# Gate and up of a spectral GEGLU block: seven products of halves instead of eight, for 256 of 448 channels and three of seven tile pairs

## The chip, the cores and the metric

The kernel runs on one core of a Trainium2 chip. The metric is the device time of one execution in microseconds (us). The engines are named as in the profile: PE is the matrix engine (PEld its weight loads), DVE the vector engine, ACT the scalar engine, POOL the GpSimd engine, SP the engine whose queue issues the transfers.

## What is computed

The input `x` has 8192 tokens of 448 channels, all in float32. `c` and `w_mod` give six rows of 448 numbers (`sa, ca, ga, sb, cb, gb`). `A` is a spectral mixer: a Fourier transform over the 8192 tokens, a small two-layer network on each frequency, and the inverse transform. `B` is a gated feed-forward network with 1792 hidden channels.

```python
h = _layernorm(x) * (1 + ca) + sa
x = x + ga * A(h)                       # rfft2, two blockwise layers, shrink, irfft2
h = _layernorm(x) * (1 + cb) + sb
x = x + gb * ((_gelu(h @ w_gate) * (h @ w_up)) @ w_down)
```

## The kernel before

The first 385 us hold the forward transform, the frequency network and the first half of the inverse transform. The rest is one loop, and the change lies in it. It has 32 iterations `i`, each over two blocks of 128 tokens. The last half of the inverse transform, the residual, the second norm and the packing of a later iteration's tokens are spread over an iteration as hooks.

An iteration has 14 steps `k` of gate and up. Step `k` computes gate and up of one tile of 128 hidden channels: `t = k // 2`, and `q = k % 2` picks tile `t` or tile `t + 7`, so a tile pair is two steps. Numbers are split into a high and a low float16 part, and a product takes high by high, high by low and low by high. The 448 channels make three tiles of 128 and one of 64, which makes 20 matmuls of 256 columns (two blocks of 128 tokens) in a step, `gu` at L1087. Two consecutive tile pairs share eight more matmuls with 64 rows: the first of the two (the "first pair") gets its results out only at its second step, after these; the second pair gets them out step by step. Since there are seven tile pairs, the odd `t` are first pairs in odd iterations and the even `t` in even iterations.

`gate_up_out` takes a result out of the accumulation bank: ACT computes the gelu of the gate half (L1123), DVE multiplies it with the up half (L1128). After both tiles of a pair POOL makes four sums of the four quarters (L1134 to L1137), since the down projection takes seven products of halves in place of eight. `quantize`, called at odd `k` for the pair before, rounds the seven operands: ACT the high part (L1145), DVE the low part (L1146).

After `k == 2` comes `down(i - 1)`: 147 matmuls of 224 columns (L1153 to L1155), with copies out by ACT (L1176, L1182), adds by DVE (L1177 to L1194), and on POOL an add (L1190) and four passes that finish the output (L1167, L1168).

The hooks for iteration `i + 2` are: at `k = 3` the inverse's inputs `g` and `v` are split into two float32r parts, the high one by ACT (L105), the low one by POOL (L107); at `k = 6` the inverse's six matmuls (L987 to L989); at 7 the residual, at 8 the statistics, at 9 and 10 the inverse square root in small DVE steps, at 11 and 12 the norm on DVE, at 13 the packing to float16. At `k = 0` SP issues the 16 transposing transfers of iteration `i + 1`.

Each engine takes its instructions in the order in which the Python code calls them; nothing reorders them. So what stands ahead of an instruction on its engine can be read from the code.

Of the kernel before, what the change touches and what calls it, by code (L numbers as in the profile page):

```python
# [19 lines left out]
D = 448  # L20
F = 1792
# [16 lines left out]
NTT = len(PKO)  # L38
LAM = 0.01
# [6 lines left out]
def spectral_geglu(ctx, tc, x, w1, b1, w2, b2, wg, wu, wd, cvec, wmod, cf1, cs2, cmi, cgm, out):  # L46
# [272 lines left out]
    with ExitStack() as bctx:  # L319
# [359 lines left out]
        def row_scales():  # L679

            GL.tensor_scalar(cb_r, cb_r, 1.0, None, op0=ALU.add)
            tiny.extend([free] * 2)
            for j, r in enumerate((cb_r, sb_r)):
                VL.tensor_reduce(rmax[:, j : j + 1], r, mybir.AxisListType.X, ALU.max, apply_absolute_value=True)
            bnd = cpool.tile([128, 1], F32, name="hb")
            VL.scalar_tensor_tensor(bnd, rmax[:, 0:1], 21.2, rmax[:, 1:2], op0=ALU.mult, op1=ALU.add)
            VL.tensor_scalar(bnd, bnd, 1.01, 1e-30, op0=ALU.mult, op1=ALU.add)
            pow2(sk, bnd)
            GL.tensor_scalar(sb_r, sb_r, sk, None, op0=ALU.mult)
            GL.tensor_scalar(cb_r, cb_r, sk, None, op0=ALU.mult)  # L690
# [48 lines left out]
        def scales1():  # L739
# [20 lines left out]
            pow2(sw, mxa)  # L760
# [122 lines left out]
        def load_g(i):  # L883
            g = ep.tile([128, CB, 128], F32, tag="g", name="g")
            dma(g, cgm[:, i * CB : (i + 1) * CB, :])
            xx = ep.tile([128, CB, D], F32, tag="xx", name="xx")
            dma(xx, xv[:, i * CB : (i + 1) * CB, :])
            nxt.setdefault(i, {}).update({"g": g, "xx": xx})
# [22 lines left out]

        def split_g(i):
            gh = ep.tile([128, CB, 128], F32R, tag="gh", name="gh")
            gl = ep.tile([128, CB, 128], F32R, tag="gl", name="gl")
            split(gh, gl, nxt[i]["g"], el=G)
            nxt[i]["g"] = gh, gl
# [32 lines left out]
    with ExitStack() as cctx:  # L949
# [7 lines left out]

        def load_d8(t):
            load_d(t, *(cp2.tile([128, n, HC], F32, tag=f"dr{n}", name="dr", bufs=2) for n in (3, 4)))
# [8 lines left out]
        def split_v(i, cs=slice(0, D)):  # L968
            n = nxt[i]
            if "vh" not in n:  # L970
                n["vh"] = cp.tile([128, CB, D], F32R, tag="vh", name="vh")
                n["vl"] = cp.tile([128, CB, D], F32R, tag="vl", name="vl")
            for b in each(i):
                split(n["vh"][:, b, cs], n["vl"][:, b, cs], n["v"][:, b, cs], el=G)

        def inverse(i, cs=slice(0, D), tag="pc"):
            nxt[i]["ps"] = []
            for b in range(CB):
                ps = bank(tag, "pi2")[:, cs]
                if i < 3:  # L980

                    T.matmul(ps, nxt[i]["g"][:, b], nxt[i]["v"][:, b, cs], start=True, stop=True)
                    nxt[i]["ps"].append(ps)
                    continue
                vh, vl = nxt[i]["vh"], nxt[i]["vl"]
                gh, gl = nxt[i]["g"]
                T.matmul(ps, gh[:, b], vh[:, b, cs], start=True, stop=False)  # L987
                T.matmul(ps, gl[:, b], vh[:, b, cs], start=False, stop=False)  # L988
                T.matmul(ps, gh[:, b], vl[:, b, cs], start=False, stop=True)  # L989
                nxt[i]["ps"].append(ps)  # L990

        def residual(i, cs=slice(0, D)):
# [3 lines left out]
            for b in range(CB):  # L996
# [34 lines left out]
        def norm2(i, b):  # L1031
            mvt, x1, r = nxt[i]["mv"], x1t[i], nxt[i]["r"][0]
            if b == 0:
                nxt[i]["n"] = cp.tile([128, CB, D], F32, tag="n2", name="n2")
            n = nxt[i]["n"]
# [9 lines left out]
        def pack_lo(i):  # L1045
# [6 lines left out]
            nts[i] = cp.tile([128, NTT, H], F16, tag="nt", name="nt", bufs=2)  # L1052
# [42 lines left out]

        def gate_up(i, k):
# [7 lines left out]
            seq = [(wh, j, j) for j in range(4)] + [(wh, j, j + 5) for j in range(3)] + [(wl, j, j) for j in range(3)]  # L1104
            for pr in range(2):
                for j, (w, tw, tn) in enumerate(seq):
                    gu(i, t, q, pr, w, full, tw, tn, first_pair and pr == 0 and j == 0, not first_pair and j == len(seq) - 1)
            if not first_pair:
                gate_up_out(i, t, q)
            elif q == 1:  # L1110
# [6 lines left out]
                for qq in range(2):  # L1117
                    gate_up_out(i, t, qq)
# [39 lines left out]
        def down(i):  # L1158
# [82 lines left out]
        }  # L1241
        inverse(0, halves[0], "pa")
# [32 lines left out]
        for i in range(nch):  # L1275
            for k in range(NFT):
# [7 lines left out]
                if i == 1:  # L1284
                    for fn, *args in second.get(k, []):
                        fn(2, *args)
                if k == 2 and i > 0:
                    down(i - 1)
                    if i == 1:
                        transposes_dma(2, range(2, NTT))  # L1290
                for fn, *args in first.pop(i * NFT + k, []):
                    fn(*args)
                if k == (3, 1, 0)[min(i, 2)] and i + 2 < nch:
                    load_v(i + 2)
                    load_g(i + 2)
                for d, fn, *args in hooks.get(k, []):
# [79 lines left out]
```

## Time and profile before

| | |
|---|---|
| time, median of 3 runs | 1942.13 us (1941.53 to 1943.13) |
| the profiled execution | 1942.27 us, its span 1940.5 us |
| PE busy | 98% of the span; weight loads 87% |
| DVE, ACT, POOL busy | 57%, 41%, 60% |
| granted PE clock, mean | 0.995 |
| gate and up, L1087 | 9856 matmuls, one of them 273 ns from start to end |
| down, L1153 to L1155 | 4704 matmuls, one of them 259 ns |

Matmuls follow each other in a pipeline, so the duration of one is longer than the distance from one start to the next; rates are read from the starts in the timeline. A row of the timeline gives the start, the length, the engine, the line, the operation, what is written and read, a count, and in brackets the idle time ahead of it and what ended that. A row of the groups gives a count, the total, the mean of one in ns, and the idle time ahead.

### The profile page before, as it was taken

The numbers are of one execution on the slowest core, as the hardware profiler recorded it, in microseconds if no ns is written. First come the engines' busy times: TensorE is split into PE (matmuls) and PEld (weight loads), VectorE is DVE, ScalarE is ACT, GpSimd is POOL, SyncE is SP. The second block draws the span as 40 slices with busy tenths as digits, with TensorE's granted clock in tenths as the row PEclk, the third lists the DMA queues.
The fourth block names the chain that finished last, engine by engine and source line by source line (L and its number), as shares of the span: only waits on it lengthen the run. The fifth ranks groups of instructions, "written<-read, shape, count | busy, mean of one in ns | idle before, by whom it ended". The sixth has DMA issues, their size and how long they took to land.

```text
span 1940.5 us, 43566 instructions
## 1 busy us (share of the span) xinstructions
PE 1901.1 (98%) x17636; PEld 1694.6 (87%) x17636; DVE 1108.7 (57%) x2352; ACT 790.1 (41%) x1342; POOL 1157.7 (60%) x1466
## 2 busy tenths in 40 slices
PE   7899999899999999999999999999999999999998
PEld 3599999778888888888888888888888888888897
DVE  8677788786555555555555555555555555555533
ACT  5587888553333333333333333333333333333322
POOL 3157655256666666666666666666666666666644
PEclk9899999999999999999999999999999999999999
DMA  9999777541111111111111111111111111111000
GB/s 351 313 286 261 194 195 196 166 125 48 44 44 44 43 43 43 43 43 44 43 44 43 43 44 43 44 44 42 45 43 44 44 43 44 43 44 44 21 16 20
DMA packets 167330, 163.35 MB, mean 84 GB/s; under 512 B 87252, under 2 KB 145496, under 8 KB 167128
## 3 DMA queue, kind: packets, MB, share of 16 engines
q1 hardware_dynamic: 167128, 160.57, 28.3%
q8 instruction: 138, 2.26, 0.5%
q14 instruction: 64, 0.52, 0.1%
HBM read 97.44 MB, written 47.25 MB: 75 GB/s over the span
## 4 chain that ended last, share of the span: by engine, by line
PE 86%; DVE 4%; ACT 3%; issue 3%; DMA 2%; POOL 1%; SPq 1%; ACTq 0%; POOLq 0%; DVEq 0%
PE pgu L1087 53%; PE pdn L1155 8%; PE pdn L1153 8%; PE pdn L1154 8%; PE ps L202 2%; DVE y L463 2%; PE pi L989 1%; PE pi L988 1%; PE pi L987 1%; POOL yl L107 1%; DVE st L163 1%; ACT th L105 0%; DMA raw<-in_B_w_gate 0%; POOL tl L107 0%; ACT zh L376 0%
## 5 line engine op out<-in xcount | busy, mean ns | idle before, releaser
L1087 PE MATMUL pgu<-nt,wh 128*128 128x256 f16 x6272 | 834.2, 273 | 0.1
L1087 PEld LDWEIGHTS <-wh 128*128 128x128 f16 x6272 | 602.7, 98 | 98.5 <-issue 31.0
L1123 ACT ACTIVATE gel<-pgu,dg 128x256 f32<-128x256 f32 x448 | 200.3, 473 | 793.2 <-PE pgu L1087 756.1
L1087 PE MATMUL pgu<-nt,wl 128*128 128x256 f16 (+1 forms) x3584 | 501.3, 272 | 0.6 <-DVE x L1128 0.6
L1155 PE MATMUL pdn<-wd,ac 128*128 128x224 f16 x1568 | 406.1, 259 | 0.2 <-DVE ac L1146 0.2
L1153 PE MATMUL pdn<-wd,ac 128*128 128x224 f16 x1568 | 406.1, 259 | 0.0
L1154 PE MATMUL pdn<-wd,ac 128*128 128x224 f16 x1568 | 406.1, 259 | 0.0
L1134 POOL TENSOR_TENSOR x<-x 128x128 f32<-128x128 f32 x223 | 239.9, 1076 | 264.0 <-DVE x L1128 230.5
L1146 DVE SCALAR_TENSOR_TENSOR ac<-x,sa_act,ac 128x896 f16<-128x896 f32 (+1 forms) x225 | 308.2, 1370 | 81.9 <-ACT ac L1145 81.9
L1087 PEld LDWEIGHTS <-wl 128*128 128x128 f16 (+1 forms) x3584 | 297.8, 97 | 57.6 <-issue 24.4
L1128 DVE TENSOR_TENSOR x<-pgu,gel 128x256 f32<-128x256 f32 x448 | 179.6, 418 | 278.7 <-ACT gel L1123 278.0
L1145 ACT ACTIVATE ac<-x,sa_act 128x896 f16<-128x896 f32 (+1 forms) x225 | 232.9, 1035 | 46.5 <-POOL x L1137 44.5
L1190 POOL TENSOR_TENSOR o<-u,p 128x224 f32<-128x224 f32 x32 | 21.0, 657 | 291.6 <-DVE u L1189 291.6
L1135 POOL TENSOR_TENSOR x<-x 128x128 f32<-128x128 f32 x223 | 158.1, 709 | 17.5
L1155 PEld LDWEIGHTS <-ac 128*128 128x128 f16 x1568 | 153.4, 98 | 0.5 <-DVE ac L1146 0.5
L1154 PEld LDWEIGHTS <-ac 128*128 128x128 f16 x1568 | 153.4, 98 | 0.4
L1153 PEld LDWEIGHTS <-ac 128*128 128x128 f16 x1568 | 153.4, 98 | 0.4
L107 POOL TENSOR_TENSOR yl<-y,yh 128x448 fp32r<-128x448 f32 x63 | 78.9, 1252 | 75.6 <-ACT yh L105 63.0
L463 DVE SCALAR_TENSOR_TENSOR y<-pm,t 64x224 f32<-64x224 f32 x256 | 99.5, 389 | 41.3 <-ACT t L455 37.4
L1136 POOL TENSOR_TENSOR x<-x 128x128 f32<-128x128 f32 x223 | 113.0, 507 | 0.0
L1137 POOL TENSOR_TENSOR x<-x 128x128 f32<-128x128 f32 x223 | 109.2, 490 | 0.0
L107 POOL TENSOR_TENSOR tl<-tr,th 128x896 f16<-128x896 f32 x30 | 57.3, 1909 | 69.5 <-DMA tr<-td 38.2
(281 smaller groups left out, 2728.4 us busy)
## 6 DMA issues: line engine op xcount, KB each, us to landing
tr<-td SPq DMA_DIRECT2D x64, 224.0 KB, 4.3
vd<-us SPq DMA_DIRECT2D x64, 224.0 KB, 3.3
xx<-in_A_x SPq DMA_DIRECT2D x32, 448.0 KB, 3.3
v<-vd SPq DMA_DIRECT2D x63, 224.0 KB, 2.7
out<-x SPq DMA_DIRECT2D x31, 448.0 KB, 2.6
xt<-in_A_x SPq DMA_DIRECT2D x15, 896.0 KB, 14.8
td<-xt SPq DMA_DIRECT2D x48, 224.0 KB, 4.3
nt<-pk SPq DMA_TRANSPOSE x480, 2.3
```

The lines of the kernel that those rows point to most:

```text
L107: (el or V).tensor_tensor(lo, src, h, ALU.subtract)
L463: V.scalar_tensor_tensor(y[ri * 64 : ri * 64 + 64, gi], pv[si, ri], LAM, tv[si, ri], op0=ALU.add, op1=ALU.min)
L1087: T.matmul(pgu[i, t, q][:, pr * H : (pr + 1) * H], w[rows, tw, f0 : f0 + 128], nts[i][rows, tn, :], start=start, stop=stop, skip_group_che ...
L1123: S.activation(gl, ps[:, :H], AF.Gelu_apprx_tanh, scale=dg)
L1128: V.tensor_tensor(dst, ps[:, H : 2 * H].rearrange("p (b c) -> p b c", b=2), gl.rearrange("p (b c) -> p b c", b=2), ALU.mult)
L1134: e.tensor_tensor(s1, a21, a22, ALU.add)
L1135: e.tensor_tensor(s2, s1, a11, ALU.subtract)
L1145: S.activation(ac[:, 0, k], x[:, k], AF.Copy, scale=sc)
L1146: V.scalar_tensor_tensor(ac[:, 1, k], x[:, k], sc, ac[:, 0, k], op0=ALU.mult, op1=ALU.subtract)
L1153: T.matmul(ps, ac[:, 0, ka], wds[t][:, 0, kb], start=t == 0, stop=False)
L1154: T.matmul(ps, ac[:, 0, ka], wds[t][:, 1, kb], start=False, stop=False)
L1155: T.matmul(ps, ac[:, 1, ka], wds[t][:, 0, kb], start=False, stop=t == NP - 1)
```

## The change

`SP = {2: 3, 4: 4, 6: 5}`: tile pairs 2, 4 and 6 take the new form from iterations 3, 4 and 5 on, which is 29 + 28 + 27 = 84 tile pairs. For these, the first 256 channels (two tiles of channels, by two blocks of tokens, by two tiles of hidden channels) are a two-by-two product of 128x128 blocks, and it is done in seven block products, each of them three matmuls of 128 columns for gate and three for up (`sp_product`). The remaining 192 channels are done as before (`rest` from tile 2 on). In `gate_up_s1` (the step `q = 0`) three products go to a bank `px` of their own; its first half `x` is copied out by ACT three times (L1211, L1214, L1219) and added onto in between. `gate_up_sums` then adds the copies on DVE (L1258, L1260, L1262) ahead of the gelu.

Four sums of the normalized tokens (`s_sums`) are made by POOL at `k = 2`, rounded by ACT and POOL (`s_pack`) and transposed by eight further transfers at `k = 3`. Sums of the weights are made once, in iterations 2 to 5 (`sp_load`, `sp_sums`, `sp_round`). The norm is written over the inverse's input `v`; therefore `v` and `g` of the next iteration are loaded at `k = 2`, after `s_sums`. The inverse is done block by block (`split_v`, `inverse1`): the splits for block 0 at `k = 3` and for block 1 at `k = 4`, the matmuls of block 0 at the end of `k = 4` and those of block 1 at the end of `k = 7`. Two powers of two that scale the float16 operands are smaller by four.

```diff
+SP = {2: 3, 4: 4, 6: 5}
...
+        def s_sums(i):
...
+            G.tensor_tensor(s[:, 0], a21, a22, ALU.add)
+            G.tensor_tensor(s[:, 1], s[:, 0], a11, ALU.subtract)
+            G.tensor_tensor(s[:, 2], a11, a21, ALU.subtract)
+            G.tensor_tensor(s[:, 3], a12, s[:, 1], ALU.subtract)
+        def s_pack(i):
...
+            S.copy(ps[:, :, 0], s[:, :4])
+            G.tensor_tensor(ps[:, :, 1], s[:, :4], ps[:, :, 0], ALU.subtract)
...
+        def gate_up_s1(i, t, first_pair):
+            pv = bank("pc", "px").rearrange("p (x r c) -> p x r c", x=2, r=2)
+            sums["px"] = pv
+            x, u = pv[:, 0], sums["u"]
+            sp_product(i, t, x, 0, 0, start=True)
+            sp_product(i, t, pv[:, 1], 3, 3)
+            S.copy(u[:, :, 0], x)
+            rest(i, t, 0, 0, first_pair, 2)
+            sp_product(i, t, x, 4, 6)
+            S.copy(u[:, :, 1], x)
+            rest(i, t, 0, 1, first_pair, 2)
+            o = outs(i, t, 0)
+            sp_product(i, t, o[:, :, 0], 1, 1, stop=not first_pair)
+            sp_product(i, t, x, 5, 4, stop=True)
+            S.copy(u[:, :, 2], x)
+            sp_product(i, t, o[:, :, 1], 2, 5, stop=not first_pair)
+        def gate_up_s2(i, t, first_pair):
+            for pr in range(2):
+                rest(i, t, 1, pr, first_pair, 2)
+            sp_product(i, t, outs(i, t, 1)[:, :, 0], 6, 2, stop=not first_pair)
...
+        def gate_up_sums(i, t, q):
+            if seven(i, t):
+                u, o = sums["u"], outs(i, t, q)
+                if q == 0:
+                    V.tensor_tensor(o, o, u[:, :, 0::2], ALU.add)
+                    y = sums["px"][:, 1].unsqueeze(2).broadcast_to([128, 2, 2, 128])
+                    V.tensor_tensor(u[:, :, 1:3], y, u[:, :, 1:3], ALU.add)
+                else:
+                    V.tensor_tensor(o, o, u[:, :, 1:3], ALU.add)
...
         hooks = {
-            0: [(1, transposes_dma)],
-            3: [(2, split_g), (2, split_v)],
-            6: [(2, inverse)],
-            7: [(2, residual)],
-            8: [(2, stats2)],
+            0: [(1, transposes_dma, range(4))],
+            3: [(1, s_transposes), (2, split_v, 0)],
+            4: [(2, inverse1, 0), (2, split_v, 1)],
+            5: [(2, residual, slice(0, D), [0])],
+            7: [(2, inverse1, 1)],
+            8: [(2, residual, slice(0, D), [1]), (2, stats2)],
...
+                if k == 2 and i > 1 and i + 1 < nch:
+                    s_sums(i + 1)
+                    s_pack(i + 1)
+                    if i + 2 < nch:
+                        load_v(i + 2)
+                        load_g(i + 2)
+                    transposes_dma(i + 1, range(4, NTT))
                 if k == 2 and i > 0:
                     down(i - 1)
...
+                if k == 3 and i > 0 and i + 2 < nch:
+                    load_xx(i + 2)
```

In an even iteration ACT stands like this before, from the end of `down` (the copy `p`) through steps 3 to 7 (`gel` is the gelu, `ac` the rounding of the pair before, `gh` and `vh` the splits):

```order
L1182 COPY p_13850<-pdn 128x224 [waits PE_49]
L1123 ACTIVATE gel<-pgu,dg 128x256 [waits DVE_49,PE_49]
L1145 ACTIVATE ac<-x_13813,sa_act 128x896 [waits Pool_49]
L105 CAST gh<-g 128x256 [waits DMAHW6_49]
L105 CAST vh<-v 128x896 [waits DMAHW5_49,DMAHW4_49]
L1123 ACTIVATE gel<-pgu,dg 128x256 [waits DVE_49,PE_49] x2
L1145 ACTIVATE ac<-x_13847,sa_act 128x896 [waits Pool_49]
```

And the same place on ACT now, steps 3 to 8, with the copies out of `px` (their destination is named `dr`):

```order
L1326 COPY p_13219<-pdn 128x224 [waits PE_49]
L1267 ACTIVATE gel<-pgu,dg 128x256 [waits DVE_49,PE_49]
L1289 ACTIVATE ac<-x_13161,sa_act 128x896
L107 CAST gh<-g 128x128 [waits DMAHW0_49]
L107 CAST vh<-v 128x448 [waits DMAHW7_49,DMAHW6_49]
L1211 COPY dr<-px 128x2x128 [waits PE_49]
L1214 COPY dr<-px 128x2x128 [waits PE_49]
L1219 COPY dr<-px 128x2x128 [waits PE_49]
L107 CAST gh<-g 128x128 [waits PE_49]
L107 CAST vh<-v 128x448 [waits Pool_49]
L1267 ACTIVATE gel<-pgu,dg 128x256 [waits DVE_49] x2
```

The three copies stand behind the gelu of the step that has just ended, the rounding `ac` and, at `t = 2`, the two splits. On PE the new form of pair 4 reads, around the place where it takes up the bank `px` again (`dr` here holds the sums of the weights; each row has its weight load ahead of it):

```order
L1113 LDWEIGHTS wh
L1113 MATMUL pgu<-nt,wh 128x256
L1113 LDWEIGHTS wl
L1113 MATMUL pgu<-nt,wl 128x256
L1192 LDWEIGHTS dr
L1192 MATMUL px<-nt,dr 128x128 [waits Activation_49]
```

The first matmul that adds onto `px` waits for ACT's first copy (L1211); everything behind it on PE waits with it. On POOL and ACT the place ahead of `down` has, now, the four sums of the tokens and their rounding `pks` between the sums of pair 0 and the output's passes; this is ACT there, with the copy `p` of `down` behind:

```order
L1267 ACTIVATE gel<-pgu,dg 128x256 [waits DVE_49,PE_49]
L1070 CAST pks<-x_13197 128x4x128 [waits DMAHW4_49,DMAHW3_49,DMAHW5_49,DMAHW2_49,DMAHW6_49,DMAHW1_49,DMAHW7_49,DMAHW0_49,Pool_49]
L1320 COPY p_13218<-pdn 128x224 [waits PE_49]
L1326 COPY p_13219<-pdn 128x224 [waits PE_49]
L1267 ACTIVATE gel<-pgu,dg 128x256 [waits DVE_49,PE_49]
```

Before, the copy `p` (L1176) came right behind the gelu. Now it comes behind a cast that waits for POOL.

More of the change, by code (lines that the diff above doesn't have):

```diff
@@ L966, in spectral_geglu, with split_v @@
         halves = [slice(0, HC), slice(HC, D)]
-        def split_v(i, cs=slice(0, D)):
+        def split_v(i, b):
             n = nxt[i]
[L970 to L974, printed above, removed]
+            for key, w in (("g", 128), ("v", D)):
+                h, l = (cp.tile([128, w], F32R, tag=key + p, name=key + p) for p in "hl")
+                split(h, l, n[key][:, b], el=G)
+                n[key + "2"] = h, l
         def inverse(i, cs=slice(0, D), tag="pc"):
@@ L995, in residual @@
             x1 = x1t[i][:, :, cs]
-            for b in range(CB):
+            for b in bs:
                 e = V if i < 3 else G
@@ L1094, in gu, with rest, seven @@
             )
+        def rest(i, t, q, pr, first_pair, j0):
+            seq = [(wh, j, j) for j in range(j0, 4)] + [(wh, j, j + 5) for j in range(j0, 3)] + [(wl, j, j) for j in range(j0, 3)]
+            for j, (w, tw, tn) in enumerate(seq):
+                last = not first_pair and not j0 and j == len(seq) - 1
+                gu(i, t, q, pr, w, full, tw, tn, first_pair and pr == 0 and j == 0, last)
+        sums_w, sums = {}, {}
+        def seven(i, t):
+            return i >= SP.get(t, nch)
@@ L1103, in gate_up @@
                         pgu[(*divmod(u, NP), qq)] = bank(tag, "pgu")
[L1104 to L1107, printed above, removed]
+            if seven(i, t):
+                (gate_up_s1, gate_up_s2)[q](i, t, first_pair)
+            else:
+                for pr in range(2):
+                    rest(i, t, q, pr, first_pair, 0)
             if not first_pair:
+                gate_up_sums(i, t, q)
                 gate_up_out(i, t, q)
```

136 lines of the change are left out of this document (109 added, 27 removed).

## Prediction

> **What bounds the kernel now.** I read the page first, then the busy time of the loop, then the timelines of PE, ACT, DVE and POOL over one odd iteration (from 1027 us) and one even one (from 1075 us).
>
> ```profile
> PE 1901.1 (98%) x17636; PEld 1694.6 (87%) x17636; DVE 1108.7 (57%) x2352; ACT 790.1 (41%) x1342; POOL 1157.7 (60%) x1466
> PE 86%; DVE 4%; ACT 3%; issue 3%; DMA 2%; POOL 1%; SPq 1%; ACTq 0%; POOLq 0%; DVEq 0%
> ```
>
> ```profile
> 400.00:1880.00 1480.00, 1477.13 (x14097) 1319.60 (x14095) 780.27 (x1548) 489.40 (x808) 948.88 (x1225) 1.00 0.15 43
> ```
>
> In the loop PE idles 2.9 us of 1480 at full clock (1.00). The other engines are used for a third to two thirds. So a matmul saved is time saved, and any wait of PE is time lost in full. The profiled execution took 1942.27 us, 0.14 above the median, 1.8 above its span; I work against 1942.27. A difference under 0.2% (3.9 us) could not be told from no change.
>
> **What PE saves.** Starts in PE's timeline:
>
> ```profile
> 1030.20 0.94 PE L1087 MATMUL pgu<-nt,wh 128*128 128x256 f16 x7
> ...
> 1031.31 0.93 PE L1087 MATMUL pgu<-nt,wh 128*128 128x256 f16 x7
> 1032.07 0.49 PE L1087 MATMUL pgu<-nt,wl 128*128 128x256 f16 x3
> 1032.40 0.93 PE L1087 MATMUL pgu<-nt,wh 128*128 128x256 f16 x7
> ```
>
> Ten matmuls of 256 columns from 1031.31 to 1032.40: 109 ns each. For 128 columns the frequency network has rows with a weight load of their own:
>
> ```profile
> 116.66 0.22 PE L370 MATMUL ps<-s,tl 128*112 128x128 f16 x1
> ...
> 117.83 0.22 PE L370 MATMUL ps<-s,tl 128*112 128x128 f16 x1
> ```
>
> Between these two stand 21 starts: 55.7 ns each. A tile pair gives up 24 x 109 = 2616 ns and gets 42 x 55.7 = 2339 ns: 277 ns less, times 84 is 23 us less.
>
> **What PE waits for: the first copy.** The new step issues two products (12 x 55.7) and four old matmuls (4 x 109), 1.10 us of work, then adds onto `px`, for which ACT must have copied it. ACT takes that copy only behind the gelu of the step just ended, the rounding `ac` and, at pair 2, two splits. Let T be the start of the pair's first matmul. For pair 2, T is 1030.20 (row above), and ACT does this:
>
> ```profile
> 1030.20 0.84 ACT L1123 ACTIVATE gel<-pgu,dg 128x256 f32<-128x256 f32 x2 [10.32 <-PE pgu L1087]
> 1030.93 1.04 ACT L1145 ACTIVATE ac<-x,sa_act 128x896 f16<-128x896 f32 x1
> 1031.86 0.40 ACT L105 CAST gh<-g 128x256 fp32r<-128x256 f32 x1
> 1032.15 0.94 ACT L105 CAST vh<-v 128x896 fp32r<-128x896 f32 x1
> 1032.99 0.48 ACT L1123 ACTIVATE gel<-pgu,dg 128x256 f32<-128x256 f32 x1
> ```
>
> The splits hold ACT for 1.13 us from 1031.86; half as wide, 0.57. So the copy starts at 1032.43, T + 2.23. Its price:
>
> ```profile
> L1176 ACT COPY p<-pdn 128x224 f32<-128x224 f32 x32 | 11.1, 346 | 114.6 <-PE pdn L1155 114.6
> ```
>
> For 256 elements about 0.37. PE goes on at T + 2.65 with 0.05 for the signal, against 1.10: a wait of 1.55 us, with little room either way (1.5 to 1.7), since nothing in it depends on DVE or POOL. For pairs 4 and 6 the starts of steps 8 and 12, and ACT:
>
> ```profile
> 1040.84 0.94 PE L1087 MATMUL pgu<-nt,wh 128*128 128x256 f16 x7
> ...
> 1050.22 0.94 PE L1087 MATMUL pgu<-nt,wh 128*128 128x256 f16 x7
> ```
>
> ```profile
> 1041.56 1.04 ACT L1145 ACTIVATE ac<-x,sa_act 128x896 f16<-128x896 f32 x1
> ...
> 1051.08 1.04 ACT L1145 ACTIVATE ac<-x,sa_act 128x896 f16<-128x896 f32 x1
> ...
> 1098.42 0.47 ACT L1123 ACTIVATE gel<-pgu,dg 128x256 f32<-128x256 f32 x1 [1.71 <-DVE rcy L118]
> 1099.23 1.04 ACT L1145 ACTIVATE ac<-x,sa_act 128x896 f16<-128x896 f32 x1 [0.34 <-POOL x L1137]
> ```
>
> The rounding starts at T + 0.72 (pair 4) and T + 0.86 (pair 6); in the even iteration at T + 1.0, as a lone gelu starts 0.2 after T. It holds ACT for 0.93 (1030.93 to 1031.86), the copy adds 0.37 and the signal 0.05. Pair 4: ready at T + 2.07; block 1 of the inverse now stands on PE ahead of it, three matmuls of 0.2, so PE arrives at 1.70: a wait of 0.35. Pair 6: ready at T + 2.21 to 2.36, PE arrives at 1.10: 1.1 to 1.25. That is with the operands of the rounding as early as now. They will be later: the rounding at these places is that of the previous pair of the new form, whose DVE adds come ahead of its gelu. Their price is bounded by
>
> ```profile
> L998 DVE TENSOR_TENSOR x<-pi,ga_r 128x448 f32<-128x448 f32 x62 | 35.7, 615 | 0.0
> L377 DVE SCALAR_TENSOR_TENSOR zl<-ps,ca,zh 112x512 fp32r<-112x512 f32 x64 | 45.8, 746 | 6.4 <-ACT zh L376 6.4
> ```
>
> so about 0.68 for 512 elements; three stand in the way of a first pair (2.0 us), one of a second pair. In the even row ACT already waits for POOL, so a delay there passes in full. Pair 6: 1.1 to 3.2; I take 2.0, between. Pair 4: 0.3 to 1.5; I take 0.7, nearer the row. The second and third copies find ACT free and are covered: 4 x 109 + 6 x 55.7 = 0.77 us of matmuls against 0.26 for the last matmul's end, 0.37 and 0.05; I take nothing, 0.05 each if not. Sum of the first copy: 29 x 1.55 + 28 x 0.7 + 27 x 2.0 = 119 us (78 to 178).
>
> **The inverse at the end of step 4.** It moves from step 6, and its third matmul needs POOL's split `vl`. POOL in the odd and in the even iteration, and PE in the even one:
>
> ```profile
> 1034.26 0.72 POOL L107 TENSOR_TENSOR gl<-g,gh 128x256 fp32r<-128x256 f32 x1
> ...
> 1082.88 0.73 POOL L107 TENSOR_TENSOR gl<-g,gh 128x256 fp32r<-128x256 f32 x1
> 1083.57 2.10 POOL L107 TENSOR_TENSOR vl<-v,vh 128x896 fp32r<-128x896 f32 x1
> ```
>
> ```profile
> 1078.07 0.93 PE L1087 MATMUL pgu<-nt,wh 128*128 128x256 f16 x7
> ```
>
> Half as wide, the splits end near 1082.88 + 0.37 + 1.1 = 1084.35, which is T + 6.3 (T = 1078.07). PE gets there after 30 x 55.7 + 8 x 109 = 2.54, the wait of 1.55 and two inverse matmuls of 0.2: T + 4.5. A wait of 1.8; in the odd iteration the splits start at T + 4.06 rather than T + 4.81 (T = 1030.20), so 1.05. I take 1.4, between, times 29: 41 us (30 to 52; nothing if the finished output's passes ahead of them on POOL came earlier, for which no row speaks).
>
> **The sums of the tokens ahead of `down`.** ACT's cast `pks` waits for four more POOL adds, and the copy `p` stands behind it:
>
> ```profile
> 1064.31 0.46 POOL L1135 TENSOR_TENSOR x<-x 128x128 f32<-128x128 f32 x1
> 1064.72 0.46 POOL L1136 TENSOR_TENSOR x<-x 128x128 f32<-128x128 f32 x1
> 1065.14 0.46 POOL L1137 TENSOR_TENSOR x<-x 128x128 f32<-128x128 f32 x1
> ```
>
> ```profile
> 1065.74 0.35 ACT L1176 COPY p<-pdn 128x224 f32<-128x224 f32 x1 [3.26 <-PE pdn L1155]
> 1068.04 0.35 ACT L1182 COPY p<-pdn 128x224 f32<-128x224 f32 x1 [1.95 <-PE pdn L1155]
> ```
>
> POOL is done with pair 0 at 1065.60; four more adds at 0.41 (the step between these) end at 1067.25, a cast of some 0.55 at 1067.8, the copy `p` at 1068.2. PE's fourth product overwrites that bank from about 1067.85. So 0.3 us are lost even if nothing else is late, and up to 1.6 when pair 6's sums are late by its DVE adds. I take 1.0, times 29: 29 us (9 to 46).
>
> The rest I cost at nothing. On SP `load_v` now waits for the sums on POOL, with eight transposes behind it, and `load_xx` and eight new transposes stand behind the output's store; all of it is used after `down` (147 matmuls, 24 of them in the 2.30 us between the two copies, so 14 us), or an iteration later. The sums of the weights are made once: 24 POOL adds of 0.46, 0 to 11 us, beside engines a third to two thirds busy. The scales are other constants. DVE's adds may hold a bank of the next pair: two adds of 0.68 in every second iteration at most, 0 to 19 us.
>
> **Sum.** 1942.3 - 23 + 119 + 41 + 29 = 2108 us.
>
> **Rivals.**
>
> *Only the bare waits.* POOL and DVE keep up: 78 for the copy, 9 for the cast, none or half for the inverse. 1942 - 23 + 78 + 9 = 2006, up to 2026. For it: PE's waits give the other engines more time. Against: the even row at 1099.23, where ACT waits for POOL already.
>
> *Faster: ACT is clear.* If the copy ended by T + 1.10, PE would not wait and the saving would stand: 1942 - 23 = 1919. The place is step `q = 0` of a new pair; the point from which it decides is ACT free at T + 0.7, and the change turns slower where a pair waits more than 0.28 on average. For it: the four old matmuls were put between for that purpose and a copy on an idle ACT (0.26 + 0.37 + 0.05) would fit. Against: the rounding begins at T + 0.72 or later in each of the rows and holds ACT 0.93.
>
> *Weight loads do not hide behind 128 columns.*
>
> ```profile
> L1087 PEld LDWEIGHTS <-wh 128*128 128x128 f16 x6272 | 602.7, 98 | 98.5 <-issue 31.0
> ```
>
> If loads of 98 ns came one after another, 42 x 98 = 4116 ns: 1.5 us more than now in place of 0.28 less, of which the 12 matmuls ahead of the wait are hidden: 2108 + 84 x (1.78 - 0.5) = 2216. Against: the 128-column rows have longer loads and still start every 55.7 ns. [...]
>
> *The clock falls in the waits.*
>
> ```profile
> 407.09 0.61 PE L1069 MATMUL ptr<-ident,pk 128*128 128x128 f16 x4 [2.27 <-ACT pk L1042]
> 407.49 1.70 PE L1087 MATMUL pgu<-nt,wh 128*128 128x256 f16 x7
> ```
>
> ```profile
> 406.00:409.00 3.00, 1.91 (x12) 1.48 (x13) 3.00 (x4) 2.61 (x4) 1.89 (x2) 0.69 0.00 0
> 409.00:412.00 3.00, 3.00 (x24) 2.44 (x23) 3.00 (x5) 2.39 (x4) 3.00 (x3) 0.75 0.82 238
> ```
>
> After an idle time of 2.27 us the clock was 0.69 and 0.75 for 6 us, a loss of 0.31 x 3 + 0.25 x 3 = 1.7 us. If each of the 27 waits at pair 6 did that: 46 us more, 2154; at all 84, 2251. Against: most of my waits are shorter. [...]
>
> **How the numbers follow.** The forecast, 2040 to 2195, has 0.62; the bare waits 0.22; the clock or the loads beyond 2195 together 0.10; faster 0.05; no difference 0.01. The range of 2000 to 2195 takes in the first two and the bounds of the terms.
>
> **What would show it.** Right: in the profile after, PE has idle time ahead of the `px` matmuls (L1192) ended by ACT L1211, over 1 us at pairs 2 and 6; ahead of L993, ended by POOL; PE's busy share well under 98%; 128-column starts 56 ns apart. Wrong: if PE's idle time in the loop stays a few us, ACT was free in time, and the first term falls.

## The result, and the profile after

The changed kernel takes 2194.38 us (2192.17 to 2197.84, 4 runs) beside 1942.02 us of the kernel before (1941.53 to 1943.13, 4 runs): a ratio of 1.130, 95% interval 1.128 to 1.132. It is slower by 252 us. The forecast was 166 us slower, and the time lies at the upper end of its range (2000 to 2195). The profiled execution has a span of 2190.4 us; before it was 1940.5.

The busy shares and the chain that ended last, from the page of the changed kernel, and the busy time of the loop (the stretch, its length, the busy time and count of PE, its weight loads, DVE, ACT and POOL, then the granted PE clock, the busy share of the transfers and GB/s):

```profile
PE 1948.9 (89%) x19148; PEld 1719.2 (78%) x19148; DVE 1273.4 (58%) x2616; ACT 895.1 (41%) x1693; POOL 1264.4 (58%) x1693
PE 27%; POOL 26%; DVE 21%; issue 8%; ACT 7%; SPq 6%; DMA 3%; POOLq 0%; ACTq 0%; DVEq 0%
```

```profile
400.00:1880.00 1480.00, 1303.58 (x13236) 1149.66 (x13235) 798.71 (x1530) 503.76 (x980) 907.04 (x1245) 0.98 0.17 44
```

PE went from 98% busy to 89%, and its share of the chain from 86% to 27%. No other engine is near full: DVE and POOL are at 58%. So nothing replaced PE as a saturated engine; a chain of short steps through four engines did; the experiments test this. What PE waited for (total, times, longest):

```profile
PE px L1192 <- ACT dr L1211: 106.3, 73, 2.4
PE pdn L1297 <- ACT p L1320: 45.1, 29, 4.2
PE pi L993 <- POOL vl L109: 16.6, 28, 0.6
PE pgu L1113 <- DVE x L1272: 12.8, 27, 2.5
PE pi L992 <- POOL gl L109: 9.6, 14, 2.5
PE px L1192 <- DVE x L1002: 9.2, 13, 0.7
PE pi L991 <- ACT vh L107: 4.1, 1, 4.1
```

The row with L1002 is not a wait for the copy. It is pair 4 of even iterations taking up its bank `px`, which the inverse used before it and which the residual on DVE gives free late.

One odd and one even iteration of PE's timeline, the rows with such a wait (pair 2 and the split; pair 6; the copy `p`; pair 2 again):

```profile
1026.35 0.49 PE L1192 MATMUL px<-nt,dr 128*128 128x128 f16 x6 [1.45 <-ACT dr L1211]
1029.33 0.47 PE L993 MATMUL pi<-vl,gh 128*128 128x448 f32 x1 [0.59 <-POOL vl L109]
...
1050.21 0.50 PE L1192 MATMUL px<-nt,dr 128*128 128x128 f16 x6 [2.42 <-ACT dr L1211]
...
1068.89 0.26 PE L1297 MATMUL pdn<-wd,ac 128*128 128x224 f16 x1 [1.49 <-ACT p L1320]
1081.70 0.50 PE L1192 MATMUL px<-nt,dr 128*128 128x128 f16 x6 [1.31 <-ACT dr L1211]
```

And the even iteration's pair 6, as the chain of waits follows it (start, length, engine, what is written, line):

```profile
1097.28 1.10 POOL x L1003
...
1098.40 0.63 DVE cst L1011
...
1099.16 0.69 DVE pgu L1258
...
1099.88 0.70 DVE dr L1260
...
1100.67 0.71 DVE pgu L1262
...
1101.47 0.48 ACT gel L1267
...
1101.97 0.44 DVE x L1272
...
1102.48 0.47 POOL x L1278
...
1103.01 1.35 POOL x L1279
1104.36 0.41 POOL x L1280
1104.78 0.42 POOL x L1281
...
1105.22 1.04 ACT ac L1289
1106.26 0.27 ACT dr L1211
```

This is the case in a dozen rows. PE's matmul of pair 6 starts at 1106.57. It waited for ACT's copy, which stood behind the rounding, which waited for POOL's sums of pair 4, which waited for DVE's multiply, the gelu, DVE's three new adds, and those for the norm's statistics and POOL's residual. Every step is short and every engine has idle time, yet the steps follow one another.

By the spans, 2190.4 - 1940.5 = 250 us are to be placed. PE's idle time rose from 39.4 (1940.5 - 1901.1) to 241.5 (2190.4 - 1948.9), by 202; its busy time by 48, although 23 were saved. Of those 71, some 29 are matmuls at a lower clock, which fell to half at 17 places of the loop (one minus the granted clock, summed over the loop, is 32 us against 3 before). About 30 more are the ends of matmuls that a wait lets run out, counted as busy: before 1026.35 two starts lie 1.73 apart, 1.62 more than the usual 0.11, where the row lists 1.45, so 0.17 a wait, 185 waits in the rows above. Some 12 us of the 71 I did not place.

### The profile page after: what moved, and what is told of

The parts are those of the page before. It is cut to its first block, busy times and chain, and to the rows that moved or that the text cites. A ratio compares the mean times of both kernels' runs of the same rounds, so it can differ in the third digit from the quotient of the medians.

```text
span 2190.4 us, 47983 instructions
## 1 busy us (share of the span) xinstructions
PE 1948.9 (89%) x19148; PEld 1719.2 (78%) x19148; DVE 1273.4 (58%) x2616; ACT 895.1 (41%) x1693; POOL 1264.4 (58%) x1693
## 4 chain that ended last, share of the span: by engine, by line
PE 27%; POOL 26%; DVE 21%; issue 8%; ACT 7%; SPq 6%; DMA 3%; POOLq 0%; ACTq 0%; DVEq 0%
PE pgu L1113 9%; SPq L1083 5%; POOL x L1279 4%; POOL x L1278 4%; PE pdn L1297 3%; PE pdn L1299 3%; PE pdn L1298 3%; DVE ac L1290 2%; DVE x L1272 2%; POOL x L1312 2%; POOL o L1311 2%; POOL x L1281 2%; POOL x L1003 2%; ACT ac L1289 2%; DVE pgu L1258 2%
## 5 line engine op out<-in xcount | busy, mean ns | idle before, releaser
L1113 PE MATMUL pgu<-nt,wh 128*128 128x256 f16 x4928 | 691.2, 275 | 2.6 <-DVE x L1272 2.5
L1113 PEld LDWEIGHTS <-wh 128*128 128x128 f16 x4928 | 467.5, 99 | 72.4 <-issue 19.3
L1113 PE MATMUL pgu<-nt,wl 128*128 128x256 f16 (+1 forms) x2912 | 441.2, 274 | 10.5 <-DVE x L1272 10.4
L1297 PE MATMUL pdn<-wd,ac 128*128 128x224 f16 x1568 | 408.5, 261 | 45.4 <-ACT p L1320 45.1
L1278 POOL TENSOR_TENSOR x<-x 128x128 f32<-128x128 f32 x223 | 168.9, 758 | 399.4 <-DVE x L1272 395.3
L1290 DVE SCALAR_TENSOR_TENSOR ac<-x,sa_act,ac 128x896 f16<-128x896 f32 (+1 forms) x225 | 300.0, 1333 | 132.1 <-ACT ac L1289 114.6
L1113 PEld LDWEIGHTS <-wl 128*128 128x128 f16 (+1 forms) x2912 | 233.5, 97 | 64.3 <-issue 33.7
L1279 POOL TENSOR_TENSOR x<-x 128x128 f32<-128x128 f32 x223 | 200.8, 900 | 17.5
L1192 PEld LDWEIGHTS <-dr 128*128 128x128 f16 x1512 | 102.1, 102 | 123.4 <-issue 122.4
L1192 PE MATMUL px<-nt,dr 128*128 128x128 f16 x1008 | 88.9, 227 | 107.8 <-ACT dr L1211 106.3
L1297 PEld LDWEIGHTS <-ac 128*128 128x128 f16 x1568 | 154.4, 98 | 1.5 <-ACT ac L1289 0.5
L1280 POOL TENSOR_TENSOR x<-x 128x128 f32<-128x128 f32 x223 | 137.2, 615 | 0.0
L1192 PEld LDWEIGHTS <-wh 128*128 128x128 f16 x1344 | 112.5, 99 | 27.5 <-issue 22.0
L1258 DVE TENSOR_TENSOR pgu<-pgu,dr 128x512 f32<-128x512 f32 x84 | 58.3, 694 | 123.1 <-PE pgu L1113 79.0
```

The lines of the kernel that those rows point to most:

```text
L1113: T.matmul(pgu[i, t, q][:, pr * H : (pr + 1) * H], w[rows, tw, f0 : f0 + 128], nts[i][rows, tn, :], start=start, stop=stop, skip_group_che ...
L1192: T.matmul(o[:, pr], weight(pr, l), act(la), start=start and pr == 0 and n == 0, stop=stop and n == 2, skip_group_check=True,)
L1278: e.tensor_tensor(s1, a21, a22, ALU.add)
L1279: e.tensor_tensor(s2, s1, a11, ALU.subtract)
L1280: e.tensor_tensor(s3, a11, a21, ALU.subtract)
L1290: V.scalar_tensor_tensor(ac[:, 1, k], x[:, k], sc, ac[:, 0, k], op0=ALU.mult, op1=ALU.subtract)
```

## The experiments

The measure beside the time is the period: the distance between the first copies `p` of two successive `down`, in the steady part of the loop, as a mean over odd and even iterations. "Clock" is one minus the granted clock, summed over the loop. The ratio is to the kernel before on the same chip.

| | us | ratio (95%) | period | clock |
|---|---|---|---|---|
| before | 1942 | | 48.25 | 3 |
| after | 2194 | 1.128 to 1.132 | 56.35 | 32 |
| 1 rounding behind the copies | 2220 | 1.142 to 1.146 | 57.5 | 51 |
| 2 casts of the sums later | 2166 | 1.114 to 1.118 | 55.7 | 32 |
| 3 inverse a step later | 2185 | 1.124 to 1.128 | 56.45 | 31 |
| 4 all three, and more | 2112 | 1.088 to 1.091 | 54.1 | 36 |
| 5 no products | 2116 | 1.088 to 1.095 | 54.6 | 86 |
| 6 a wait filled | 2195 | 1.130 to 1.134 | 56.3 | 11 |
| 7 as 4, norm behind pair 6 | 2076 | 1.069 to 1.074 | 53.0 | 39 |
| 8 norm behind pair 6 alone | 2308 | 1.188 to 1.193 | 60.9 | 86 |
| 9 no products, inverse later | 1978 | 1.018 to 1.022 | 49.3 | 6 |
| 10 as 3, matmuls only | 1992 | 1.025 to 1.029 | 49.0 | 13 |
| 11 as 3, no adds | 2029 | 1.044 to 1.048 | 50.25 | 15 |
| 12 as 7, norm behind `down` | 2336 | 1.200 to 1.206 | 61.3 | 157 |

**1. The rounding behind the copies.** `quantize` of a pair ahead of a new one is called one step later.

```diff
+        held = []
...
+                if held:
+                    quantize(*held.pop())
                 if k % 2 == 1 and i + k > 1 and (i, k) != (nch - 1, NFT - 1):
-                    quantize(*((i, k // 2 - 1) if k > 1 else (i - 1, NP - 1)))
+                    held.append((i, k // 2 - 1) if k > 1 else (i - 1, NP - 1))
+                    if not seven(i, k // 2 + 1):
+                        quantize(*held.pop())
```

> At the three places the rounding ac (L1289 of the changed kernel) is called after the new step, so on ACT the three copies stand ahead of it. Theory (ACT's order sets the wait): PE's idle time ended by the first copy falls from 106 us to 15 to 30, what is left at pair 2 behind the two splits; the waits at down and at the inverse stay; the time falls by 80 to 110 us, to about 2095. Rival (the operands come late from DVE and POOL, and the rounding only hands their lateness on): the wait comes back at PE's banks or at down's last operand, and the time stays above 2150.

2219.95 us, 25 more than after the change, as the rival had it. What PE waited for:

```profile
PE pgu L1113 <- DVE x L1272: 85.7, 62, 3.1
PE pdn L1297 <- ACT p L1320: 40.7, 20, 4.2
PE px L1192 <- ACT dr L1211: 31.2, 39, 1.6
```

The wait for the copy fell from 106.3 to 31.2: ACT's order did hold the copy. But the rounding's low half now stands on DVE ahead of the next pair's adds and multiplies, and PE waits for the banks that those release (85.7, before 12.8). The wait changed its place: PE's idle time is nearly the same (245.2 us, before 241.5). Of the 25 us some 18 are further falls of the clock (51 us lost, before 32).

**2. The casts of the sums later.** `s_pack` goes from ahead of `down` to the end of step 5, its transposes to step 6.

```diff
-                    s_pack(i + 1)
...
-            3: [(1, s_transposes), (2, split_v, 0)],
+            3: [(2, split_v, 0)],
...
+            5: [(1, s_pack), (2, residual, slice(0, D), [0])],
+            6: [(1, s_transposes)],
```

> The rounding of the token sums (the cast pks and its POOL half) moves from ahead of down to the end of step 5, its transposes from step 3 to step 6. Theory (the cast that waits for POOL holds ACT's copy p): PE's 45 us at the start of down's fourth product go, and 40 to 60 us of the time with the clock, to about 2145. Rival (the copy p is late by the gelu or the rounding ahead of it): the wait stays over 30 us and the time within 15 us of 2194.

2165.79 us, 29 less. The wait for the copy `p` fell from 45.1 to 2.3, so the cause is the theory's, yet a third of that came back, 14 us, in the wait for the copy of `px` (106.3 to 120.6), and the time stayed 21 us above the forecast of 2145.

**3. The inverse a step later.** Its first block, the second block's split and the first residual go one step on.

```diff
-            4: [(2, inverse1, 0), (2, split_v, 1)],
-            5: [(2, residual, slice(0, D), [0])],
+            5: [(2, inverse1, 0), (2, split_v, 1)],
+            6: [(2, residual, slice(0, D), [0])],
```

> Block 0 of the inverse, the split of block 1 and the residual of block 0 come one step later (5, 5 and 6). Theory (POOL's split ends some 6 us after step 3, whatever PE does): PE gets there 1.2 to 1.8 us later, its 26 us at the inverse fall under 8, and the time by 15 to 30, to about 2172. Rival (the split waits for PE or for its transfer, and moves with it): 26 us stay, time 2194.

2185.36 us, 9 less; the waits for the split hardly moved (15.0 for `vl` and 14.7 for `gl`, before 16.6 and 9.6), as the rival had it.

**4. All of these together.** The rounding as in 1; `s_pack` after `down`; split, inverse and residual two steps on or one, statistics and root of the norm one step on.

```diff
...
+            4: [(2, split_v, 0)],
+            6: [(2, inverse1, 0), (2, split_v, 1)],
+            7: [(2, residual, slice(0, D), [0])],
+            8: [(2, inverse1, 1)],
+            9: [(2, residual, slice(0, D), [1]), (2, stats2)],
+            10: [(2, rsqrt_part, 5), (2, rsqrt_part, 9)],
...
```

> The rounding ac after the copies, the rounding of the token sums after down, the split of block 0 after the copies of pair 2, the inverse's two blocks at the end of steps 6 and 8, the residual, statistics and inverse square root one step later. Theory (the waits add up and the saving of 23 us is real): PE idles 10 to 30 us in the loop, the clock is back at 0.99 or more, and the time is 1925 to 1950. Rival (DVE and POOL as a chain bound the loop with the added work): above 2000.

2112.48 us: 82 less than after the change, and 172 more than the kernel before on that chip (1940.41). The rival's number came. What is left for PE is one large wait, again for banks:

```profile
PE pgu L1113 <- DVE x L1272: 96.0, 50, 3.1
```

In the timeline of DVE the multiplies that release these banks stand behind the statistics, the nine root steps, the norm's four passes and the new adds of pair 6.

**5. No products.** `SP = {}`: all pairs in the old form, everything else as changed.

```diff
-SP = {2: 3, 4: 4, 6: 5}
+SP = {}
```

> No pair takes the seven products (the table of pairs is empty), so the three pairs are computed with eight products as before, and the loads, sums and roundings of the weights for them are gone; the norm, the inverse in two blocks, the sums and the casts of the activations stay where the change put them. Theory (the trace of the changed kernel adds up: its waits are those of the products plus those of the moved norm): from 2194 us go the waits of the px matmuls, 106 us behind ACT and 9 us behind DVE, their drains (some 84 x 0.2 = 17 us), the wait for banks (13 us) and the 32 us of halved clock less a third; PE's own saving of 23 us is lost again. That is about 2055 us, between 2035 and 2075, and the wait of down for the copy p stays near 45 us. Rival (the moved norm is what crowds DVE and POOL, and the products merely show it): over 2100 us, with the waits in other places.

2116.32 us, so without products the moves cost 178 us, against 70 in the forecast. The time is the rival's, its reason is not: in the loop PE waits in one place only, at the end of step 4. The waits, and the granted clock (last number but two) behind one of them:

```profile
PE pi L992 <- POOL gl L109: 58.8, 28, 2.5
PE pi L993 <- POOL vl L109: 13.8, 28, 0.6
```

```profile
1156.00:1159.00 3.00, 2.40 (x8) 1.38 (x9) 0.00 (x0) 0.76 (x2) 1.79 (x4) 0.55 0.71 190
1159.00:1162.00 3.00, 3.00 (x16) 2.03 (x14) 0.00 (x0) 0.00 (x0) 1.03 (x1) 0.50 0.16 31
```

**9. No products, and the inverse a step later.** The edits of 3 and 5.

> No seven products, and the first block's inverse, the second block's split and the first residual one step later, as in the kernel with the inverse later. Theory (without products the moves cost only PE's wait of some 2.8 us for POOL's split at the end of step 4, and the two halved clock windows behind it, 3.3 us an iteration): both go, about 29 x 6 us: 1955 us, 1940 to 1975, with the granted clock above 0.99. Rival (the moved work crowds POOL or DVE, and PE waits somewhere else): above 2050 us.

1977.78 us, just outside the theory's bounds, with its mechanism: the 58.8 us for `gl` are gone, the wait for `vl` stays (17.6), the clock is whole (6 us lost, not 86). From 5 to 9 the time fell by 138, which is the 58.8 and the 80 of clock. So without products the early inverse costs 138 us; with them it costs 9 (3). A wait's price depends on who is late already.

**10 and 11. The products taken apart.** Both have the edit of 3. Run 10 has the matmuls of the seven products without ACT's copies and DVE's adds; run 11 has matmuls and copies. Both leave out terms of the result, and serve for the time alone.

```diff
-            S.copy(u[:, :, 0], x)
...
-                    V.tensor_tensor(o, o, u[:, :, 0::2], ALU.add)
-                    y = sums["px"][:, 1].unsqueeze(2).broadcast_to([128, 2, 2, 128])
-                    V.tensor_tensor(u[:, :, 1:3], y, u[:, :, 1:3], ALU.add)
...
-                    V.tensor_tensor(o, o, u[:, :, 1:3], ALU.add)
```

> The kernel before it in this list with the matmuls of the seven products in the three pairs, but without ACT's copies of their shared product and without DVE's adds of them, so that the pairs' sums lack these terms; the weight sums of the first iterations are made as well. Theory (the 128-column matmuls run every 56 ns, the saving of PE stands): 23 us under the kernel without products, give or take 10 for the weight sums. Rival (a matmul of 128 columns with its own weight load, or the change between shapes, costs more than its 56 ns): the same time or more.

> As the kernel with the matmuls only, with ACT's three copies a pair put back and DVE's adds still left out. Beside the kernel with the inverse later (2185 us), which has the adds too, it parts the cost of the products into ACT's and DVE's. Theory one (the wait is ACT's order: the copy stands behind the rounding, the rounding behind POOL's sums): PE waits for the copy nearly as in the full change, 60 us or more above the kernel with matmuls only. Theory two (it is the chain through DVE: two adds of 0.69 us stand ahead of each gelu, so multiply, POOL's sums, rounding and copy come that much later): within 30 us of the kernel with matmuls only, and the rest up to 2185 us comes with the adds.

With 9 and 3 they make a ladder: 1978, matmuls +15, copies +36, adds +157, 2185. The matmuls' +15 is made of two parts. In four early iterations, in which the weight sums are loaded, made and rounded, the copies `p` stand 218 us apart (498 to 716) where run 9 has 196 (497 to 693): 22 us. From there on an iteration takes 49.0 in place of 49.3. So the time is the rival's, but not for its reason. The matmuls themselves run as forecast; of 12 in a row, the first and the matmul after the last, here of the changed kernel:

```profile
1103.07 0.28 PE L1192 MATMUL px<-nt,wh 128*128 128x128 f16 x2
...
1103.74 0.49 PE L1113 MATMUL pgu<-nt,wh 128*128 128x256 f16 x3
```

0.67 us for 12, 56 ns each; in run 10 they start 56 ns apart too. Of the saving of 0.83 us an iteration 0.3 shows in the period. A wait of 0.34 for the copy `p` in every second iteration takes a part of it; the rest was not placed. Run 11 has the wait for the copy with hardly a delay ahead of ACT:

```profile
PE px L1192 <- ACT dr L1211: 54.1, 54, 1.5
```

It is the bare wait of the forecast's first term, about half of it. What doubles it, and spreads to everything else, are DVE's adds. They take three times 84 x 0.69 us, 175 in all, and the time rises by 157 with them, though DVE is busy for 54% of run 11. From run 3 to run 11 not one wait fell but several: for the copy of `px` from 98.6 to 54.1, for `p` from 51.3 to 13.6, for the split from 29.7 to 0.8, for banks from 14.3 to 0.4. Of run 11's two theories neither has the 36 us of the copies (60 or more, up to 30); that most of the cost comes with the adds is theory two's.

**6. A wait filled.** Eighteen matmuls into an unread bank, at pair 6 only.

```diff
+            if t == 6:
+                pz = bank("pd", "pz")
+                for j in range(18):
+                    T.matmul(pz[:, :H], wh[:, 0, :128], nts[i][:, 0, :], start=True, stop=True)
             sp_product(i, t, x, 4, 6)
```

> In pair 6 alone, eighteen matmuls of 256 columns into a bank that nobody reads stand ahead of the product that waits 2.2 to 2.4 us for ACT's copy. They fill some 2.0 us of that wait and add no result. Theory (the clock is halved for 3.4 us because PE stood idle just before): the fall after pair 6 goes, some 13 of the 19 falls, 1.7 us each: about 2172 us, 2165 to 2178, and the granted clock is back above 0.985. Rival one (the falls don't come from that wait): 2190 to 2200 us with the clock at 0.982. Rival two (the fill is longer than the wait and delays the chain): over 2200 us.

2195.05 us: no change. Yet the edit did what it should. Pair 6 in PE's timeline (L1216 are the fillers), the same stretch by engines, and PE's largest waits (L1301 is the line of L1297):

```profile
1106.44 2.13 PE L1216 MATMUL pz<-nt,wh 128*128 128x256 f16 x18
1108.85 0.50 PE L1192 MATMUL px<-nt,dr 128*128 128x128 f16 x6 [0.28 <-ACT dr L1211]
```

```profile
1106.00:1109.00 3.00, 2.72 (x29) 2.30 (x26) 2.76 (x13) 1.32 (x3) 1.47 (x3) 1.00 0.00 0
```

```profile
PE px L1192 <- ACT dr L1211: 54.4, 70, 1.9
PE pdn L1301 <- ACT p L1324: 54.1, 29, 4.2
```

The wait of pair 6 is 0.28 in place of 2.23 and no fall follows; over the loop the clock loses 11 us, not 32. Some 27 x 2 = 54 us of matmuls were added, 21 us of clock were won back, and the period is the same to 0.1 us. Neither expectation allowed for that. The matmuls themselves could be free, as they lie in a wait that PE had anyway. The clock that came back should have saved time if PE's pace set it, and it did not: PE waited again, 9 us of it at the copy `p` (45.1 to 54.1), which hangs on POOL and ACT.

**7 and 8. The second norm out of the way of pair 6.** Statistics and root after step 13, the scaling in the next iteration's step 0, the casts in step 1. Run 7 does this to 4, run 8 to the changed kernel.

```diff
...
+            0: [(1, norm2, 0), (1, norm2, 1)],
+            1: [(1, pack_hi), (1, pack_lo), (1, transposes_dma, range(4))],
...
+            13: [(2, stats2), (2, rsqrt_part, 5), (2, rsqrt_part, 9)],
```

> The kernel with all four moves, and beside them the second norm as well: its statistics and reciprocal root come after step 13 instead of in steps 9 and 10, the scaling in step 0 and the casts and transposes in step 1 of the next iteration. Theory (what was left in the kernel with all moves, per two iterations waits of 1.4, 3.1 and 1.8 us for DVE's multiplies and two clock falls of 1.7 us, comes from the norm's DVE work of some 9 us standing between the multiplies and adds of pairs 5 and 6): they go, 10.3 us per two iterations of 108.8: about 1970 us, 1950 to 2010. Rival (DVE, ACT and POOL form one chain that is simply too long; the wait moves to the next steps): 2080 us or more.

> The changed kernel with that move of the second norm alone: rounding, casts of the sums and inverse stay. Theory one (ACT reaches the copy of px late because DVE does the norm ahead of the adds and multiplies, so that POOL's sums and the rounding behind them are late): the px wait at pair 6 falls by about half, 29 x 1.2 = 35 us, and most falls of the clock go with it, 20 us: about 2140 us. Theory two (it is ACT's own order, the rounding ahead of the copy, whatever DVE does): 2185 to 2200 us with the px wait near 106 us.

Run 7, 2076.04 us, is the fastest of the full computation in the new form, and 7% slower than before; run 8, 2308.07 us, is 114 slower than the change itself. Run 7 came out as its rival said, the wait moved on, if 4 us below the rival's 2080. The wait for banks is gone and another took its place:

```profile
PE pdn L1299 <- DVE ac L1290: 82.0, 32, 3.4
```

The norm on DVE now stands ahead of the last rounding that `down` needs. In run 8, where the rounding is as early as in the change, the same:

```profile
PE pdn L1297 <- ACT p L1320: 104.5, 29, 4.3
PE px L1192 <- ACT dr L1211: 80.7, 71, 1.9
PE pdn L1299 <- DVE ac L1290: 52.3, 30, 3.0
```

The wait for the copy did fall (106.3 to 80.7), and more than that came up in `down`. Theory one of run 8 falls as to its sum, theory two as to the wait.

**12. The norm behind `down`.** To 7: the scaling at the end of step 2, casts in 3, sums in 4, their casts in 5, their transposes in 6.

```diff
...
+            2: [(1, norm2, 0), (1, norm2, 1)],
+            3: [(1, pack_hi), (1, pack_lo), (1, transposes_dma, range(4))],
+            4: [(1, s_sums), (1, transposes_dma, range(4, NTT)), (2, split_v, 0)],
+            5: [(1, s_pack)],
+            6: [(1, s_transposes), (2, inverse1, 0), (2, split_v, 1)],
...
```

> The whole change, with its vector work in another order: all four moves of the earlier kernel (the rounding behind the copies, the casts of the sums later, split and inverse later), the second norm's statistics and root after step 13, its scaling after the products of down in step 2, its casts in step 3, the sums in step 4, their casts in step 5 and transposes in step 6. Theory (the chain is one of order: once nothing but the pair's own adds stands ahead of its multiply and of its rounding, PE waits for the split alone): the wait of 82 us in down and the falls of the clock behind it go: 1970 us, 1950 to 2010, still above the kernel before by the first iterations' weight sums (about 22 us) and the split's wait. Rival (the adds make the chain too long in any order, and the wait moves once more): 2040 us or more.

2335.85 us, the slowest. The wait in `down` did go (82.0 to 5.5), but PE and SP's queue show a new one, and the wait for the copy of `px` is back at pair 2:

```profile
PE pi L991 <- ACT vh L107: 147.0, 29, 8.2
PE px L1192 <- ACT dr L1211: 92.5, 28, 3.6
```

```profile
SPq L900 <- ACT pk L1045: 559.4, 28, 35.2
SPq L900 <- POOL x L1065: 201.7, 28, 9.2
```

The norm lies in the buffer of the inverse's input. So the load of the next `v` (L900) waits on SP until the casts and sums have read the norm; the load of `g` stands behind it, and the split and the inverse come late. The place that the change gave the norm ties its end to the next load: there is a latest step for it, and by then DVE is full.

## Why the forecast came out as it did

*The direction and the waits it named* were right, and so were most of their sizes. Pair 2: forecast 1.55, the rows show 1.45 and 1.31 with 0.17 of a matmul's end. Pair 6: 2.0, shown 2.42 and 2.23. Pair 4: 0.7, shown 0.26 or less but for the last two iterations; in even iterations PE waited 0.70 ahead of that pair, for its bank (9.2 in all), and for that the forecast has no term. All waits for the first copy: 119, shown 106.3; by pairs 45, 20 and 54, shown 38.8, 6.4 and 61.1. The term's lower bound, 78, comes to 82 by its own figures. The inverse: 41, shown 16.6 + 9.6 + 4.1, or 30. Here the forecast miscounted: a new step `q = 0` has six products, 36 matmuls of 128 columns and not 30, by which its own rows give waits of 1.45 and 0.7, and 31 us. The casts ahead of `down`: 29, shown 45.1, of which three waits of about 4 in the iterations that make the weight sums. An add: 0.68, shown 0.69. A matmul of 128 columns: 55.7 ns, shown 56; the rival of loads that do not hide is out.

*What was left out of the sum*: the ends of matmuls (about 30 us), the falls of the clock (29; a rival of its own, and it came true at 17 places, though winning 21 us of it back in run 6 saved nothing), banks held by the adds (12.8, forecast 0 to 19 and taken as nothing) and by the residual (9.2), and the weight sums (run 10: 22 us, forecast 0 to 11 and taken as nothing).

*The number.* The three terms came to 182 us where the forecast had 189. With the saving of 23 that makes 159 of the 252 us; the other 93 lie in what was left out. That the time still lies in the range, by 0.6 us, is luck: the upper end is the sum of the terms' highest values (1942.3 - 23 + 178 + 52 + 46), and only the casts came near theirs.

*The step that failed* is the first one: "a matmul saved is time saved, and any wait of PE is time lost in full". It held for the kernel before, with PE at 98%. The sum then added waits as if it went on holding. After the change it does not: 21 us of clock won back at pair 6 saved nothing (6); a wait removed comes back in part (2) or in full elsewhere (1, 8); the early inverse costs 138 us or 9 according to what stands around it (5 and 9, after and 3). So the split of the cost was wrong, too: the forecast put 119 on the products' copies and 70 on the moves. On the chip no one split holds. With the inverse early the moves cost 178 us and the products 78 on top (5, after); with the inverse a step later the moves cost 37 and the products 207 (9, 3). Of the 207 the adds on DVE, which the forecast priced only as a delay of the rounding and a bank held, are 157 (3, 11).

*The rivals.* "Only the bare waits" assumed that POOL and DVE keep up; run 11, without the adds and with the inverse later, is the nearest to that case, at 2029 (forecast up to 2026), with 22 us of weight sums in it that the forecast left out. "ACT is clear" needed ACT free at T + 0.7; at pairs 2 and 6 the copies came 1.3 to 2.4 us late.

*What stays open*: whether any order of the vector work gets the 23 us. Each order tried moved the wait. Whether the adds would cost as much on an engine or at a place of their own was not tried.

## What to carry to other kernels

A sum of waits holds while the engine that waits is the bound; where the waits come to a share like the 11% here, follow the chain through the other engines, and count each step added to it at its full length, however idle its engine looks. Before an exchange of matmuls for vector work, ask what else is queued on the engines between one result and the bank that it releases. To price a part, remove it with the rest in place: the same wait cost 138 us alone and 9 in company.

## What the runs showed of the hardware

**The falls of the clock lie on a grid of 3.413 us.** At 1047.79 (1050.21 - 2.42) PE fell idle for 2.42 us and kept its clock; at 1104.34 it fell idle for 2.23 and the clock was halved. The busy time of the changed kernel in stretches of 3.41 us, laid so that the fall fills one:

```profile
1045.06:1048.48 3.42, 2.47 (x29) 1.55 (x27) 2.30 (x5) 2.21 (x4) 2.29 (x4) 1.00 0.00 0
1048.48:1051.89 3.41, 1.68 (x27) 1.63 (x27) 3.13 (x14) 1.71 (x4) 0.88 (x2) 1.00 0.00 0
...
1103.09:1106.50 3.41, 1.25 (x18) 1.04 (x16) 3.20 (x12) 1.90 (x4) 2.10 (x3) 0.99 0.00 0
1106.50:1109.92 3.42, 3.35 (x29) 3.08 (x29) 3.28 (x8) 0.77 (x3) 2.25 (x3) 0.51 0.00 0
```

The longer wait is cut by a boundary of these stretches and leaves 1.68 us of work in its own; the shorter lies in one stretch, with 1.25. All 17 falls of this run's loop start within 0.02 us of one grid of 3.413 us; 15 of them last one stretch, two last two (6.83 us). The 21 falls of run 4 lie as closely on a grid of their own. On these grids, falls followed stretches with at most 1.44 us of busy PE in this run and at most 1.60 in run 4, and no new fall followed a stretch with over 1.7. The bound is not sharp: a stretch with 1.43 us in this run and one with 1.58 in run 4 were followed by none. No stretch ahead of a fall of this run was without work: the emptiest had 0.17 us of busy PE.

**A short add on POOL took 1.35 us (median) beside DVE's rounding and 0.46 with DVE idle.** In the chain above L1279 takes 1.35 us where its neighbours take 0.41 to 0.47. DVE, in its timeline, runs the rounding's low half at that time:

```profile
1102.90 1.15 DVE L1290 SCALAR_TENSOR_TENSOR ac<-x,sa_act,ac 128x896 f16<-128x896 f32 x1 [0.51 <-ACT ac L1289]
```

Over the run L1279 takes 0.45 to 1.42 us. It took 0.46 or less each of the 46 times when DVE was idle throughout; the 132 times when it ran beside an L1290 it took 1.35 (median) and ended 0.31 after it (median). In 27 of these the L1290 started less than 0.05 us ahead of the add; there the add took 0.46 and the L1290 1.44 (medians) in place of 1.15. What ties the two to each other no run shows. The two meet in the kernel before as well, where mostly the first of the four sums, L1134, meets the rounding's low half and takes 1.29 us (median); there PE did not wait for it.
